# Attention values with the probabilities stationary and V moving, and queries as 512-wide matmuls, in a one-token decode block

## The chip, the core and the metric

The kernel runs on one core of a Trainium2 chip. The metric is the device time of one execution in microseconds (us). The kernel before takes 207.13 us, the median of three runs (206.97, 207.13 and 207.15).

## The reference

One token passes through a transformer block: layer norm, attention over a cache of 4096 positions with 32 heads of 128 (every query head has its own keys and values), an output projection with a residual, a second layer norm, and a gated feed-forward with GELU and a second residual. Inputs and output are bf16.

```
h  = x + attention(layernorm(x))            # x: [1, 1, 640]
q  = (layernorm(x) @ wq)                    # 32 heads x 128
p  = softmax(q . k_cache / sqrt(128))       # k_cache, v_cache: [1, 32, 4096, 128]
o  = p @ v_cache                            # 32 heads x 128
h  = x + o @ wo                             # wo: [4096, 640]
h2 = h + (gelu(n @ w_gate) * (n @ w_up)) @ w_down,   n = layernorm(h)     # 640 -> 1728 -> 640
```

The two caches are 33.5 MB each, and the weights together some 17 MB; each byte is read once.

## The kernel before

The 32 heads are taken in `NG = 8` groups of `HG = 4`. Within a group, head h owns the 32 partitions 32h to 32h+31, and each partition holds `R = 128` consecutive positions of its head. So a group's K (or V) is one tile of 128 partitions x 128 rows x 128 numbers, 4 MB, fetched by one transfer. There are two buffers for K (`kbuf`) and two for V (`vbuf`).

A class `Sched` keeps one list of operations for each engine, in the order in which the Python code calls it, and adds the semaphore waits; every engine runs its list strictly in that order. All large transfers are issued by SyncE (SP) in one list, so a transfer whose buffer is not free holds back those listed behind it. The order of the loop is this: `query(0)`, `scores(0)`, `query(1)`, `softmax(0)`, and then for g = 0 to 7: `scores(g+1)`, `query(g+2)`, `softmax(g+1)`, `values(g)`, the load of K(g+3), the load of V(g+2). The parts are:

- `query(g)` (L281, L285): for each head five matmuls multiply the normed x (`xb`, copied to 32 columns) with 128 columns of `wq`, so that the head's q stands in each of its 32 partitions; ScalarE copies the result to `qb`.
- `scores(g)`: four pieces of 32 rows. `mult` (L296, VectorE) multiplies K with q into `prod`, one of three buffers; `fold` (L305, TensorE) adds up 128 numbers to 16 by eight accumulating matmuls with the identity, 512 columns each; `red` (L312, VectorE) sums the 16 that are left. VectorE's order is mult 0, mult 1, red 0, mult 2, red 1, mult 3, red 2, red 3. The buffer of K is free (`kfree`) after mult 3.
- `softmax(g)`: the maximum over each group by way of VectorE and two small matmuls (L329 to L337), then the exponentials on ScalarE (L344) into `P4`: 128 partitions x 128 rows x 4 columns, in which only the column of the partition's own head is not zero. The sums of a partition are collected in `RS`.
- `values(g)` (L351): 128 matmuls, one for each row r. V's row (128 x 128) is the stationary operand, loaded anew each time, and the 4 columns of `P4` move; the result for four heads accumulates in 4 columns of `po`. The buffer of V is free (`vfree`) after it.

After the last group, TensorE sums `RS` (L370), VectorE inverts it (L372) and scales `po` (L407), TensorE transposes (L408), VectorE copies it out (L409), and four matmuls with `sel` bring the heads' outputs into the order of `wo` (L412). 160 matmuls with one moving column make the output projection (L422), then come the residual (L426), the second layer norm, gate and up projection (L454, 70 matmuls each, into `pg` and `pu`), GELU, and 56 matmuls of the down projection (L477).

The weights of the second half have no memory of their own: `wo` lies over `wq` (free after the last query), `wg` and `wu` over the two K buffers, `wd` over the V buffer of group 6. In SP's list the last V (group 7, in three pieces) waits for values(5), and behind it stand `wo`, `wg` (K of group 6 used), `wu` (K of group 7 used) and `wd` (values(6) done).

Of the kernel before, what the change touches and what calls it, by code (L numbers as in the profile page):

```python
# [5 lines left out]
FP32 = mybir.dt.float32  # L6
BF16 = mybir.dt.bfloat16
ALU = mybir.AluOpType
ACTF = mybir.ActivationFunctionType
AX = mybir.AxisListType  # L10

D = 640
H = 32
DH = 128
SK = 4096
DF = 1728
NC_D = D // 128
# [5 lines left out]
HG = 4  # L23
NG = H // HG
PPH = 128 // HG
R = SK // PPH
RP = 32
NP = R // RP
NFT = 13
NF = NFT + 1  # L30
WD_PARTS = (6, 4, 2, 1)

WD_COLS = []
for _n in WD_PARTS:
    _b = 128 * len(WD_COLS)
    WD_COLS += [(_b, _n, _i) for _i in range(_n)]
FREM = DF - NFT * 128

# [66 lines left out]
def bass_sequential_preLN__gqa_block_cached__glu_gated_geglu__decode_kernel(  # L105
# [12 lines left out]
    S = Sched(nc)  # L118

    def sb(name, shape, dt):  # L120
        return nc.alloc_sbuf_tensor(name, shape, dt)
# [5 lines left out]
    vbuf = [sb("vbuf%d" % i, [128, R, DH], BF16) for i in range(2)]  # L127

    def over(name, base, shape):
        return nc.alloc_sbuf_tensor_at(name, shape, BF16, offset=nc.lookup_mloc(base).addr)  # L130

    wq_sb = over("wq_sb", arena, [128, NC_D, H * DH])
# [7 lines left out]
    qb = sb("qb", [128, NG, DH], BF16)  # L140
    sc = [sb("sc%d" % i, [128, R], FP32) for i in range(2)]
    P4 = [sb("P4_%d" % i, [128, R, HG], BF16) for i in range(2)]
    RS = sb("RS", [128, H], FP32)
    mx = sb("mx", [128, NG], FP32)
    mrow = sb("mrow", [1, H], FP32)
    nb = sb("nb", [128, H], FP32)
    rz = sb("rz", [128, H], FP32)
    aT = sb("aT", [128, H], BF16)
    aH = sb("aH", [H, DH], BF16)
    aP = sb("aP", [128, H], BF16)  # L150
    x_sb = sb("x_sb", [128, NC_D], BF16)
    x32 = sb("x32", [128, NC_D], FP32)
# [1 line left out]
    sq = sb("sq", [128, NC_D], FP32)  # L154
    st = sb("st", [128, 4], FP32)
    ln = sb("ln", [128, 12], FP32)
    xb = sb("xb", [128, NC_D, PPH], BF16)
    hln = sb("hln", [128, NC_D], BF16)
    g_t = sb("g_t", [128, NF], FP32)
    t1 = sb("t1", [128, NF], FP32)  # L160
# [11 lines left out]
    ones = sb("ones", [128, 128], FP32)  # L172
    ones_bf = sb("ones_bf", [128, 128], BF16)
    I32 = sb("I32", [128, 128], FP32)
    Ibf = sb("Ibf", [128, 128], BF16)
# [4 lines left out]
    pq = nc.alloc_psum_tensor("pq", [128, 512], FP32)  # L180
    pm = nc.alloc_psum_tensor("pm", [128, 512], FP32)
    po = nc.alloc_psum_tensor("po", [128, 512], FP32)
    pz = nc.alloc_psum_tensor("pz", [128, 512], FP32)
    pg = nc.alloc_psum_tensor("pg", [128, 512], FP32)
    pu = nc.alloc_psum_tensor("pu", [128, 512], FP32)


    t_one = S.op("vector", lambda v: v.memset(ones[:, :], 1.0))
# [13 lines left out]
        e4[:, :], I32[:, :].rearrange("p (j i) -> p j i", j=4), axis=AX.X), [t_i32])  # L202
    t_m32 = S.op("vector", lambda v: v.reduce_sum(
        m32[:, :], I32[:, :].rearrange("p (j i) -> p i j", j=4), axis=AX.X))
    t_sel = None
    for j in range(4):
        t_sel = S.op("gpsimd", lambda g, j=j: g.affine_select(
# [4 lines left out]
    d_wq = S.dma("sync", "wq", lambda s: s.dma_start(  # L212
        wq_sb[:, :, :], A_wq[:, :].rearrange("(p c) n -> p c n", c=NC_D)))
# [4 lines left out]
    d_k, d_v = [None] * NG, [None] * NG  # L218
    kfree, vfree = [None] * NG, [None] * NG

    def load_k(g):
        d_k[g] = S.dma("sync", "k%d" % (g % 2), lambda s: s.dma_start(
            kbuf[g % 2][:, :, :], cache(A_k_cache, g)), [kfree[g - 2] if g >= 2 else None])
# [23 lines left out]
    def layernorm(src, t_src, o, dst, ps, beside=None):  # L247
# [19 lines left out]

    t_x32 = S.op("vector", lambda v: v.tensor_copy(x32[:, :], x_sb[:, :]), [d_x])  # L268
    t_xb = layernorm(x32, t_x32, 0, (
        xb[:, :, :], x32[:, :].unsqueeze(2).to_broadcast([128, NC_D, PPH])), pz)  # L270


    t_qb = [None] * NG

    def query(g):
        tok = None
        for hh in range(HG):
            for c in range(NC_D):
                n0 = (g * HG + hh) * DH
                last = hh == HG - 1 and c == NC_D - 1  # L280
                tok = S.op("tensor", lambda t, hh=hh, c=c, n0=n0: t.matmul(  # L281
                    pq[hh * PPH:(hh + 1) * PPH, 0:DH], xb[:, c, :], wq_sb[:, c, n0:n0 + DH],
                    start=(c == 0), stop=(c == NC_D - 1)),
                    [t_xb, d_wq, t_qb[g - 1] if g else None], token=last)
        t_qb[g] = S.op("scalar", lambda a: a.copy(qb[:, g, :], pq[:, 0:DH]), [tok])  # L285
        return tok


    fold_done, red_done = {}, {}
    t_exp, t_pv = [None] * NG, [None] * NG  # L290
    n_piece = 0
    t_qlast = None

    def mult(g, s):
        n = g * NP + s
        return S.op("vector", lambda v: v.tensor_tensor(  # L296
            out=prod[n % NPR][:, :, :], in0=kbuf[g % 2][:, s * RP:(s + 1) * RP, :],
            in1=qb[:, g, :].unsqueeze(1).to_broadcast([128, RP, DH]), op=ALU.mult),
            [d_k[g], t_qb[g], fold_done.get(n - NPR)])

    def fold(g, s, t_mult):
        n = g * NP + s
        W = 512 // RP
        for j in range(DH // W):
            fold_done[n] = S.op("tensor", lambda t, j=j: t.matmul(  # L305
                pf[n % 2][:, :], Ibf[:, :], prod[n % NPR][:, :, j * W:(j + 1) * W],
                start=(j == 0), stop=(j == DH // W - 1)),
                [t_mult, t_ibf, red_done.get(n - 2)], token=(j == DH // W - 1))

    def red(g, s):  # L310
        n = g * NP + s
        red_done[n] = S.op("vector", lambda v: v.reduce_sum(  # L312
            sc[g % 2][:, s * RP:(s + 1) * RP],
            pf[n % 2][:, :].rearrange("p (r w) -> p r w", r=RP), axis=AX.X),
            [fold_done[n], t_exp[g - 2] if g >= 2 else None])

    def scores(g):
        for s in range(NP):
            tm = mult(g, s)
            if s == NP - 1:  # L320
                kfree[g] = tm
            fold(g, s, tm)
            if s >= 1:
                red(g, s - 1)
        red(g, NP - 1)

    def softmax(g):

# [18 lines left out]
                [e, t_p4[g % 2], t_rs, t_pv[g - 2] if g >= 2 else None])  # L347

    def values(g):
        for r in range(R):  # L350
            t_pv[g] = S.op("tensor", lambda t, r=r: t.matmul(  # L351
                po[:, g * HG:(g + 1) * HG], vbuf[g % 2][:, r, :], P4[g % 2][:, r, :],
                start=(r == 0), stop=(r == R - 1)), [t_exp[g], d_v[g][r]], token=(r == R - 1))
        vfree[g] = t_pv[g]

    query(0)
    scores(0)
    query(1)
    softmax(0)
    load_k(2)  # L360
    load_v(1)
    for g in range(NG):
        if g + 1 < NG:
            scores(g + 1)
            if g + 2 < NG:
                t_qlast = query(g + 2)
            softmax(g + 1)
        if g == NG - 1:

            z = S.op("tensor", lambda t: t.matmul(pz[:, 0:H], ones[:, :], RS[:, :], start=True, stop=True),  # L370
                 [t_exp[NG - 1]])
            t_rz = S.op("vector", lambda v: v.reciprocal(rz[:, :], pz[:, 0:H]), [z])  # L372
        values(g)
        if g + 3 < NG:
            load_k(g + 3)
        if g + 2 < NG:
            load_v(g + 2)


    def pieces(slot, dst, src, cuts, waits):  # L380
# [14 lines left out]
    d_wdr = S.dma("sync", "wdr", lambda s: s.dma_start(  # L395
        wd_sb[0:FREM, NFT, :], B_w_down[NFT * 128:DF, :]), [vfree[NG - 2]])
    d_wd = []
    for i, n in enumerate(WD_PARTS):
        s0 = len(d_wd)
        tok = S.dma("sync", "wd%d" % i, lambda s, s0=s0, n=n: s.dma_start(  # L400
            wd_sb[:, s0:s0 + n, :],
            B_w_down[128 * s0:128 * (s0 + n), :].rearrange("(p i) n -> p i n", i=n)), [vfree[NG - 2]])
# [1 line left out]
    d_wd.append(d_wdr)  # L404


    a = S.op("vector", lambda v: v.tensor_mul(aT[:, :], po[:, 0:H], rz[:, :]), [t_rz, t_pv[NG - 1]])  # L407
    a = S.op("tensor", lambda t: t.matmul(pm[0:H, 0:128], aT[:, :], Ibf[:, :], start=True, stop=True), [a])  # L408
    a = S.op("vector", lambda v: v.tensor_copy(aH[:, :], pm[0:H, 0:128]), [a])  # L409
    b = None  # L410
    for j in range(4):
        b = S.op("tensor", lambda t, j=j: t.matmul(  # L412
# [6 lines left out]
    for c in range(H):  # L419
        for cc in range(NC_D):  # L420
            last = c == H - 1 and cc == NC_D - 1
            b = S.op("tensor", lambda t, c=c, cc=cc, last=last: t.matmul(  # L422
                pp[:, cc:cc + 1], wo_sb[:, c, cc::NC_D], aP[:, c:c + 1],
                start=(c == 0 and cc == 0), stop=last, skip_group_check=True),
# [19 lines left out]
    def up(ps, w, d_w, t0):  # L444
        b = None
        for c in range(NC_D):
            for s in range(NF):
                first = c == 0 and s == 0
                last = c == NC_D - 1 and s == NF - 1
                rows, cols = FREM, slice(NFT * 128, DF)  # L450
                if s < NFT:
                    b0, n, k = WD_COLS[s]
# [8 lines left out]
    a = S.op("vector", lambda v: v.tensor_copy(g_t[:, :], pg[:, 0:NF]), [t_g])  # L461
    a = S.op("vector", lambda v: v.tensor_mul(t1[:, :], g_t[:, :], g_t[:, :]), [a])
    a = S.op("vector", lambda v: v.tensor_mul(t2[:, :], t1[:, :], g_t[:, :]), [a])
    a = S.op("vector", lambda v: v.scalar_tensor_tensor(
        out=t3[:, :], in0=t2[:, :], scalar=GELU_C1, in1=g_t[:, :], op0=ALU.mult, op1=ALU.add), [a])
    a = S.op("scalar", lambda a: a.activation(e_t[:, :], t3[:, :], ACTF.Exp, scale=-2.0 * GELU_C0), [a])
    a = S.op("vector", lambda v: v.tensor_scalar(d_t[:, :], e_t[:, :], 1.0, 0.0, ALU.add, ALU.add), [a])
    a = S.op("vector", lambda v: v.reciprocal(r_t[:, :], d_t[:, :]), [a])
    a = S.op("vector", lambda v: v.tensor_mul(gu[:, :], g_t[:, :], r_t[:, :]), [a])
    t_hm = S.op("vector", lambda v: v.tensor_mul(hm[:, :], gu[:, :], pu[:, 0:NF]), [a, t_u])  # L470

    order = [NFT] + list(range(NFT))
    for i, s in enumerate(order):
        kk = FREM if s == NFT else 128
        for j in range(4):
            last = i == NF - 1
            b = S.op("tensor", lambda t, s=s, j=j, kk=kk, last=last: t.matmul(  # L477
                pd[32 * j:32 * j + 1, 0:NQ], hm[0:kk, s:s + 1], wd_sb[0:kk, s, j * NQ:(j + 1) * NQ],
                start=False, stop=last, skip_group_check=True),
# [40 lines left out]
```

## Time and profile before

| What | us |
|---|---|
| median of the runs | 207.13 |
| span of the profiled execution, first to last instruction | 205.4 |
| TensorE busy, matmuls | 135.3 (66%) |
| TensorE busy, weight loads (beside matmuls) | 78.5 (38%) |
| VectorE busy | 103.4 (50%) |
| ScalarE busy | 24.5 (12%) |
| transfers | 84.48 MB, mean 411 GB/s |
| mean granted TensorE clock | 0.790 |

The profile's own record of the execution is its span, 205.4 us; the time of a run, 207.13 us in the median, holds some 1.7 us more around the program's instructions. A step in the profile that moves the last instruction moves the time by as much. The busy time of a matmul holds its passage through the array, so matmuls that follow each other closely overlap in it; how fast they really follow is read from stretches of many.

### The profile page before, as it was taken

How to read it: one execution, taken by the hardware profiler on the slowest of the kernel's cores; microseconds unless marked ns; L12 is line 12 of the kernel's file. 1: busy time of each engine (PE TensorE's matmuls, PEld its weight loads, DVE VectorE, ACT ScalarE, POOL GpSimd, SP SyncE). 2: the span in 40 equal slices, each digit the busy share in tenths (PEclk: the TensorE clock that was granted, in tenths of full speed). 3: DMA queues.
4: the chain of work that ended last, by engine and by line, in shares of the span. 5: the costliest groups of instructions: out<-in, count | busy, mean ns of one | idle time of the engine just before them, and what ended most of it. 6: DMA issues, size and time to landing. Idle time of an engine off the chain costs nothing.

```text
span 205.4 us, 3993 instructions
## 1 busy us (share of the span) xinstructions
PE 135.3 (66%) x1847; PEld 78.5 (38%) x1847; DVE 103.4 (50%) x118; ACT 24.5 (12%) x86; POOL 2.2 (1%) x11
## 2 busy tenths in 40 slices
PE   0003049758698889684978598857777767687883
PEld 0002013223282373254326333712262237676771
DVE  2003087698685757925782777188627940001120
ACT  2001000040040050022004000500040004000000
POOL 3000000000000000000000000000000000000000
PEclk9999999978967975995599559959995995555555
DMA  7999999999999999999999999999999999999981
GB/s 247 439 431 408 434 453 440 408 434 456 427 415 424 440 440 413 421 443 426 434 421 440 424 427 434 431 437 415 440 427 431 399 422 424 423 416 422 397 336 46
DMA packets 4712, 84.48 MB, mean 411 GB/s; under 512 B 664, under 2 KB 856, under 8 KB 1880
## 3 DMA queue, kind: packets, MB, share of 16 engines
q1 hardware_dynamic: 4552, 84.23, 96.6%
q8 instruction: 14, 0.23, 0.5%
q10 hardware_dynamic: 144, 0.00, 0.0%
q14 instruction: 2, 0.02, 0.0%
HBM read 84.23 MB, written 0.00 MB: 410 GB/s over the span
## 4 chain that ended last, share of the span: by engine, by line
DMA 60%; DVE 21%; PE 13%; SPq 4%; issue 1%
DMA kbuf<-in_A_k_cache_dram 49%; DVE prod L296 16%; PE pf L305 11%; DMA wd_sb<-in_B_w_down_dram 10%; DVE sc L312 4%; SPq L400 4%; PE po L351 2%; PE pm L331 0%; PE pf L477 0%; DVE mx L329 0%; PE pz L370 0%; SPq L212 0%; PE pm L337 0%; SPq L395 0%; DVE o_sb L481 0%
## 5 line engine op out<-in xcount | busy, mean ns | idle before, releaser
L305 PE MATMUL pf<-prod,Ibf 128*128 128x512 bf16 x256 | 76.8, 461 | 33.7 <-DVE prod L296 33.6
L296 DVE TENSOR_TENSOR prod<-kbuf,qb 128x4096 bf16<-128x4096 bf16 x32 | 72.4, 2283 | 24.7 <-DMA kbuf<-in_A_k_cache_dram 24.7
L305 PEld LDWEIGHTS pf<-prod,Ibf 128*128 128x128 bf16 x256 | 27.4, 115 | 80.0 <-DVE prod L296 42.4
L312 DVE TENSOR_REDUCE sc<-pf 128x32 f32<-128x512 f32 x32 | 22.0, 688 | 24.3 <-PE pf L305 24.3
L351 PE MATMUL po<-P,vbuf 128*128 128x4 bf16 x1024 | 28.1, 165 | 2.0 <-issue 2.0
L351 PEld LDWEIGHTS po<-P,vbuf 128*128 128x128 bf16 x1024 | 27.5, 101 | 2.2 <-issue 2.1
L344 ACT ACTIVATE P<-sc,nb 32x128 bf16<-32x128 f32 x32 | 18.6, 581 | 0.9
L285 ACT CAST qb<-pq 128x128 bf16<-128x128 f32 x8 | 2.1, 265 | 103.4 <-PE pq L281 103.4
L251 PE MATMUL pz<-st,ones 128*128 128x2 f32 x4 | 1.2, 363 | 17.7 <-DVE st L250 17.7
L422 PE MATMUL pf<-aP,wo_sb 128*128 128x1 bf16 x160 | 7.0, 179 | 1.7 <-issue 1.3
L344 ACT ACTIVATION_READ_ACCUMULATOR P<-sc,nb 32x1 f32 x32 | 8.1, 254 | 0.0
L251 PEld LDWEIGHTS pz<-st,ones 128*128 128x128 f32 x4 | 1.0, 311 | 17.8 <-DVE st L250 17.8
L422 PEld LDWEIGHTS pf<-aP,wo_sb 128*128 128x128 bf16 x160 | 6.7, 131 | 2.1 <-issue 1.5
L268 DVE CAST x<-x_sb 128x5 f32<-128x5 bf16 x1 | 0.2, 172 | 14.1 <-DMA x_sb<-in_A_x_dram 14.1
L281 PE MATMUL pq<-wq_sb,xb 128*32 128x128 bf16 x160 | 5.7, 232 | 1.7 <-DVE xb L265 1.7
L331 PE MATMUL pm<-I,mx 128*1 128x128 f32 x16 | 3.0, 270 | 4.6 <-DVE mx L329 4.6
L281 PEld LDWEIGHTS pq<-wq_sb,xb 128*32 128x32 bf16 x160 | 4.2, 101 | 4.8 <-issue 3.0
L337 PE MATMUL pm<-mrow,ones 1*128 1x4 f32 x16 | 3.0, 258 | 3.0 <-DVE mrow L334 3.0
L262 ACT ACTIVATE ln<-ln 128x1 f32<-128x1 f32 x2 | 0.4, 203 | 35.1 <-DVE ln L260 35.1
L340 ACT ACTIVATE nb<-pm 128x4 f32<-128x4 f32 x8 | 1.4, 173 | 26.4 <-PE pm L337 26.4
L426 DVE TENSOR_TENSOR h<-x,pf 128x5 f32<-128x5 f32 x1 | 0.2, 161 | 8.6 <-PE pf L422 8.6
L337 PEld LDWEIGHTS pm<-mrow,ones 1*128 1x128 f32 x16 | 2.3, 182 | 5.3 <-DVE mrow L334 5.3
(59 smaller groups left out, 38.1 us busy)
## 6 DMA issues: line engine op xcount, KB each, us to landing
kbuf<-in_A_k_cache_dram SPq DMA_DIRECT2D x8, 4096.0 KB, 26.2
vbuf<-in_A_v_cache_dram SPq DMA_DIRECT2D x7, 4096.0 KB, 29.2
wq_sb<-in_A_wq_dram SPq DMA_DIRECT2D x1, 5120.0 KB, 15.4
wo_sb<-in_A_wo_dram SPq DMA_DIRECT2D x2, 1920.0 KB, 26.6
vbuf<-in_A_v_cache_dram SPq DMA_DIRECT2D x1, 2048.0 KB, 16.2
vbuf<-in_A_v_cache_dram SPq DMA_DIRECT2D x1, 1536.0 KB, 19.5
wg_sb<-in_B_w_gate_dram SPq DMA_DIRECT2D x1, 1296.0 KB, 32.8
wu_sb<-in_B_w_up_dram SPq DMA_DIRECT2D x1, 1296.0 KB, 30.1
```

What stands on the lines that cost most here:

```text
L251: c = S.op("tensor", lambda t: t.matmul(ps[:, 0:2], ones[:, :], st[:, o:o + 2], start=True, stop=True), [b, t_one])
L281: tok = S.op("tensor", lambda t, hh=hh, c=c, n0=n0: t.matmul(pq[hh * PPH:(hh + 1) * PPH, 0:DH], xb[:, c, :], wq_sb[:, c, n0:n0 + DH], star ...
L285: t_qb[g] = S.op("scalar", lambda a: a.copy(qb[:, g, :], pq[:, 0:DH]), [tok])
L296: return S.op("vector", lambda v: v.tensor_tensor(out=prod[n % NPR][:, :, :], in0=kbuf[g % 2][:, s * RP:(s + 1) * RP, :], in1=qb[:, g, :]. ...
L305: fold_done[n] = S.op("tensor", lambda t, j=j: t.matmul(pf[n % 2][:, :], Ibf[:, :], prod[n % NPR][:, :, j * W:(j + 1) * W], start=(j == 0) ...
L312: red_done[n] = S.op("vector", lambda v: v.reduce_sum(sc[g % 2][:, s * RP:(s + 1) * RP], pf[n % 2][:, :].rearrange("p (r w) -> p r w", r=R ...
L331: b = S.op("tensor", lambda t: t.matmul(pm[0:1, 0:128], mx[:, g:g + 1], I32[:, :], start=True, stop=True), [a, t_i32, t_exp[g - 1] if g el ...
L337: d = S.op("tensor", lambda t: t.matmul(pm[:, 256:256 + HG], ones[0:1, :], mrow[0:1, g * HG:(g + 1) * HG], start=True, stop=True), [c])
L344: t_exp[g] = S.op("scalar", lambda a, lo=lo, hi=hi, h=h, hh=hh: a.activation(P4[g % 2][lo:hi, :, hh], sc[g % 2][lo:hi, :], ACTF.Exp, bias= ...
L351: t_pv[g] = S.op("tensor", lambda t, r=r: t.matmul(po[:, g * HG:(g + 1) * HG], vbuf[g % 2][:, r, :], P4[g % 2][:, r, :], start=(r == 0), s ...
L400: tok = S.dma("sync", "wd%d" % i, lambda s, s0=s0, n=n: s.dma_start(wd_sb[:, s0:s0 + n, :], B_w_down[128 * s0:128 * (s0 + n), :].rearrange ...
L422: b = S.op("tensor", lambda t, c=c, cc=cc, last=last: t.matmul(pp[:, cc:cc + 1], wo_sb[:, c, cc::NC_D], aP[:, c:c + 1], start=(c == 0 and ...
```

## The change

`query(g)`: the normed x is copied to 128 columns, and five matmuls make all four heads' q at once, 512 columns wide, in all 128 partitions. ScalarE picks each head's 128 columns for its 32 partitions in four copies.

`values(g)`: the operands change places. Four rows of `P4` (128 x 16) are stationary and the four rows of V (128 x 512) move; 32 such matmuls accumulate a 16 x 512 result. Of its 16 x 4 blocks of 128 only those where the row of P equals the row of V are wanted. So there is a new step, `extract(g)`: VectorE multiplies the result with a mask (`rmask`) and sums over the four rows, and a small matmul with `gsel` (TensorE) sums the four rows' heads into 32 x 128 (`pa`), where the eight groups accumulate. `extract(g)` stands in VectorE's and TensorE's lists within scores(g+2), behind the third piece; the last two stand ahead of and behind values(7). The result has two PSUM buffers, `po` and `pg`, and `pu` becomes `pa`. The transpose at the end is gone, since the heads are rows of `pa` already, and the division by the sum becomes one scaling per head.

```diff
+VR = 4
+VM = VR * HG
...
     def query(g):
         tok = None
+        for c in range(NC_D):
+            n0 = g * HG * DH
+            tok = S.op("tensor", lambda t, c=c, n0=n0: t.matmul(
+                pq[:, :], xb[:, c, :], wq_sb[:, c, n0:n0 + HG * DH],
+                start=(c == 0), stop=(c == NC_D - 1)),
+                [t_xb, d_wq, t_qb[g - 1] if g else None], token=(c == NC_D - 1))
         for hh in range(HG):
-            for c in range(NC_D):
-                n0 = (g * HG + hh) * DH
-                last = hh == HG - 1 and c == NC_D - 1
-                tok = S.op("tensor", lambda t, hh=hh, c=c, n0=n0: t.matmul(
-                    pq[hh * PPH:(hh + 1) * PPH, 0:DH], xb[:, c, :], wq_sb[:, c, n0:n0 + DH],
-                    start=(c == 0), stop=(c == NC_D - 1)),
-                    [t_xb, d_wq, t_qb[g - 1] if g else None], token=last)
-        t_qb[g] = S.op("scalar", lambda a: a.copy(qb[:, g, :], pq[:, 0:DH]), [tok])
+            lo, hi = hh * PPH, (hh + 1) * PPH
+            t_qb[g] = S.op("scalar", lambda a, lo=lo, hi=hi, hh=hh: a.copy(
+                qb[lo:hi, g, :], pq[lo:hi, hh * DH:(hh + 1) * DH]), [tok])
         return tok
...
             if s >= 1:
                 red(g, s - 1)
+            if s == 2 and g >= 2:
+                extract(g - 2)
         red(g, NP - 1)
+
+    def extract(g):
+        a = S.op("vector", lambda v: v.tensor_tensor(
+            out=xm[:, :, :], in0=pv[g % 2][0:VM, :].rearrange("p (r d) -> p r d", r=VR),
+            in1=rmask[:, :].unsqueeze(2).to_broadcast([VM, VR, DH]), op=ALU.mult), [t_pv[g], t_gsel])
+        t_ext[g] = S.op("vector", lambda v: v.reduce_sum(
+            xz[g % 2][:, :], xm[:, :, :].rearrange("p r d -> p d r"), axis=AX.X),
+            [a, t_acc[g - 2] if g >= 2 else None])
+        t_acc[g] = S.op("tensor", lambda t: t.matmul(
+            pa[0:H, 0:DH], gsel[:, :, :].rearrange("p g x -> p (g x)")[:, g * H:(g + 1) * H], xz[g % 2][:, :],
+            start=(g == 0), stop=(g == NG - 1), skip_group_check=True), [t_ext[g]])
...
     def values(g):
-        for r in range(R):
-            t_pv[g] = S.op("tensor", lambda t, r=r: t.matmul(
-                po[:, g * HG:(g + 1) * HG], vbuf[g % 2][:, r, :], P4[g % 2][:, r, :],
-                start=(r == 0), stop=(r == R - 1)), [t_exp[g], d_v[g][r]], token=(r == R - 1))
+        n = R // VR
+        for i in range(n):
+            r = i * VR
+            t_pv[g] = S.op("tensor", lambda t, i=i, r=r: t.matmul(
+                pv[g % 2][0:VM, :], P4[g % 2][:, r:r + VR, :], vbuf[g % 2][:, r:r + VR, :],
+                start=(i == 0), stop=(i == n - 1)),
+                [t_exp[g], d_v[g][r], t_ext[g - 2] if g >= 2 else None], token=(i == n - 1))
         vfree[g] = t_pv[g]
...
-            z = S.op("tensor", lambda t: t.matmul(pz[:, 0:H], ones[:, :], RS[:, :], start=True, stop=True),
+            z = S.op("tensor", lambda t: t.matmul(pz[0:H, 0:1], RS[:, :], ones[:, 0:1], start=True, stop=True),
                  [t_exp[NG - 1]])
-            t_rz = S.op("vector", lambda v: v.reciprocal(rz[:, :], pz[:, 0:H]), [z])
+            t_rz = S.op("vector", lambda v: v.reciprocal(rz[:, :], pz[0:H, 0:1]), [z])
+            extract(NG - 2)
         values(g)
...
-    a = S.op("vector", lambda v: v.tensor_mul(aT[:, :], po[:, 0:H], rz[:, :]), [t_rz, t_pv[NG - 1]])
-    a = S.op("tensor", lambda t: t.matmul(pm[0:H, 0:128], aT[:, :], Ibf[:, :], start=True, stop=True), [a])
-    a = S.op("vector", lambda v: v.tensor_copy(aH[:, :], pm[0:H, 0:128]), [a])
+    extract(NG - 1)
+    a = S.op("vector", lambda v: v.tensor_scalar(
+        aH[:, :], pa[0:H, 0:DH], rz[:, 0:1], 0.0, ALU.mult, ALU.add), [t_rz, t_acc[NG - 1]])
```

At the start four small VectorE operations more build `rmask`, `hsel` and `gsel`, and the last step of the first layer norm writes 640 columns of `xb` in place of 160.

More of the change, by code (lines that the diff above doesn't have):

```diff
@@ L146, in bass_sequential_preLN__gqa_block_cached__glu_gated_geglu__decode_kernel @@
     nb = sb("nb", [128, H], FP32)
-    rz = sb("rz", [128, H], FP32)
-    aT = sb("aT", [128, H], BF16)
+    rz = sb("rz", [H, 1], FP32)
+    xm = sb("xm", [VM, VR, DH], FP32)
+    xz = [sb("xz%d" % i, [VM, DH], FP32) for i in range(2)]
+    rmask = sb("rmask", [VM, VR], FP32)
+    hsel = sb("hsel", [VM, HG], FP32)
+    gsel = sb("gsel", [VM, NG, H + HG], FP32)
     aH = sb("aH", [H, DH], BF16)
@@ L156, in bass_sequential_preLN__gqa_block_cached__glu_gated_geglu__decode_kernel @@
     ln = sb("ln", [128, 12], FP32)
-    xb = sb("xb", [128, NC_D, PPH], BF16)
+    xb = sb("xb", [128, NC_D, 128], BF16)
     hln = sb("hln", [128, NC_D], BF16)
@@ L185, in bass_sequential_preLN__gqa_block_cached__glu_gated_geglu__decode_kernel @@
     pu = nc.alloc_psum_tensor("pu", [128, 512], FP32)
+    pv = [po, pg]
+    pa = pu
     t_one = S.op("vector", lambda v: v.memset(ones[:, :], 1.0))
@@ L204, in bass_sequential_preLN__gqa_block_cached__glu_gated_geglu__decode_kernel @@
         m32[:, :], I32[:, :].rearrange("p (j i) -> p i j", j=4), axis=AX.X))
+    S.op("vector", lambda v: v.reduce_sum(
+        rmask[:, :], I32[0:VM, 0:VM].rearrange("p (j h) -> p j h", h=HG), axis=AX.X))
+    t_hs = S.op("vector", lambda v: v.reduce_sum(
+        hsel[:, :], I32[0:VM, 0:VM].rearrange("p (j h) -> p h j", h=HG), axis=AX.X))
+    t_gs = S.op("vector", lambda v: v.memset(gsel[:, :, :], 0.0))
+    t_gsel = S.op("vector", lambda v: v.tensor_copy(
+        gsel[:, :, 0:HG], hsel[:, :].unsqueeze(1).to_broadcast([VM, NG, HG])), [t_hs, t_gs])
     t_sel = None
@@ L269, in bass_sequential_preLN__gqa_block_cached__glu_gated_geglu__decode_kernel @@
     t_xb = layernorm(x32, t_x32, 0, (
-        xb[:, :, :], x32[:, :].unsqueeze(2).to_broadcast([128, NC_D, PPH])), pz)
+        xb[:, :, :], x32[:, :].unsqueeze(2).to_broadcast([128, NC_D, 128])), pz)
     t_qb = [None] * NG
@@ L290, in bass_sequential_preLN__gqa_block_cached__glu_gated_geglu__decode_kernel @@
     t_exp, t_pv = [None] * NG, [None] * NG
+    t_ext, t_acc = [None] * NG, [None] * NG
     n_piece = 0
```

## Prediction

> **What bounds the kernel now.** I read the page's slices first, then the chain of waits in order of time, then the timeline, and last the granted clock in stretches.
>
> ```profile
> PEclk9999999978967975995599559959995995555555
> DMA  7999999999999999999999999999999999999981
> L351 PE MATMUL po<-P,vbuf 128*128 128x4 bf16 x1024 | 28.1, 165 | 2.0 <-issue 2.0
> ```
>
> The transfers are busy in every slice but the first and the last two: the kernel streams memory, and compute lies beside it. The 1024 value matmuls are to be seen here with 28.1 us. In the chain of waits (start, us, what):
>
> ```profile
> 87.00 27.25 DMA kbuf<-in_A_k_cache_dram
> ...
> 126.06 27.05 DMA kbuf<-in_A_k_cache_dram
> 153.11 0.02 issue
> 153.13 2.30 DVE prod L296
> 155.43 0.05 issue
> 155.48 3.61 PE pf L305 x8
> 159.08 0.02 issue
> 159.11 0.69 DVE sc L312
> ...
> 168.99 3.42 PE po L351 x128
> ...
> 180.78 21.48 DMA wd_sb<-in_B_w_down_dram
> 202.26 0.04 issue
> ```
>
> K of group 5 lands at 114.24 and K of group 7 at 153.11: a group (K and V) takes the transfers (153.11 - 114.24) / 2 = 19.44 us. That is the pace to beat. The end is the last weight transfer at 202.26 and 3 us behind it. The timeline gives the matmuls' real pace, and what stands behind them:
>
> ```profile
> 162.06 1.90 PE L305 MATMUL pf<-prod,Ibf 128*128 128x512 bf16 x8 [0.74 <-DVE prod L296]
> 164.86 1.90 PE L305 MATMUL pf<-prod,Ibf 128*128 128x512 bf16 x8 [0.90 <-DVE prod L296]
> 168.92 3.49 PE L351 MATMUL po<-P,vbuf 128*128 128x4 bf16 x128
> 172.28 0.61 PE L370 MATMUL pz<-RS,ones 128*128 128x32 f32 x2
> 175.46 2.96 PE L351 MATMUL po<-P,vbuf 128*128 128x4 bf16 x105 [1.98 <-issue]
> ```
>
> Eight 512-column matmuls take 1.90 us at full clock, of which some 0.17 is the last one's passage: 0.216 us each. At half clock (155.48 above) eight take 3.61, so 0.43 each. A group's value matmuls follow each other at 3.49 / 128 = 0.027 us.
>
> **The change, part by part.** *Values.* 128 x 0.027 = 3.5 us become 32 matmuls of 512 columns. No row has 16 stationary columns. Bounds: 0.027 each (the issue pace of L351), so 0.9 us a group; and 0.43 (cold fold), so 13.7. I take 0.216, the warm fold, which has the same moving operand: 6.90 us a group.
>
> The Trainium skill, "TensorE: Matmul & The Clock Gate", section "Back-to-back issue gap", gives about 131 ns for a sustained 512-column matmul. The rows measure 216 for it; by 131 ns values would be 4.2 us and the loop 17.2, under the transfers' pace.
>
> *Extract.* No row has these two VectorE operations; both read 512 f32 in each partition, as red does (L312, 0.69, and 0.60 from start to start). Multiply 0.69, 0.02, sum 0.60 until mult 3 starts: 1.31 us. Bounds: 0.9 (the multiply at mult's 2.28 / 4096 for each number) and 1.6 (at 0.97 ns, from the xb row's 0.44 for 160 and hln's 0.29 for 5). It stands in VectorE's list between red 1 and mult 3; mult 3, fold 3, the softmax and the values behind them all come later by it. The small f32 matmul costs as L331, 0.38, and lies between fold 2 and fold 3, where TensorE waits for mult 3 anyway.
>
> *The loop.* TensorE's list closes a circle: values(g), fold 0 of g+2, and softmax(g+2), which stands ahead of values(g+1). VectorE can't run ahead of fold 0, as red 0 stands before mult 2. From the rows: fold 0 1.92 (warm, with its semaphore); from red 0's start (159.11) to the next values (168.92) 9.81; extract 1.31; values 6.90. Sum 19.94 us, over the transfers' 19.44. Before, it was 3.3 + 1.92 to 3.6 + 9.81 = 15.0 to 16.7, so TensorE waited for K. Compute now sets the pace, by half a microsecond a group; and the head start that compute has is used up at once, since the circle closes from values(0) on. That starts at 56.82 in the timeline, when the first two groups' scores are done, which the change leaves alone. So values(0) has issued its last matmul at 56.82 + 6.90 = 63.7, and values(6) at 63.7 + 6 x 19.94 = 183.4. Before it was 172.3.
>
> *Queries.* 20 matmuls in 0.67 us become five of 0.216, 1.08 us, right behind fold 3. The softmax's first matmul starts 3.0 us after fold 3 does (167.86 - 164.86), and 1.73 + 1.08 = 2.81 is inside: nothing. Four copies of 0.27 in place of one are done about 4.06 after fold 3's start, and ScalarE's next (nb, 169.03) comes 4.17 after: nothing, and only exponentials with a whole loop of room stand behind it. At the start, the wider xb (0.5 to 0.9), the query at half clock (2.2) and the copies (1.1) fall into the 6.7 us for which the first mult waits for K; the mask setup falls into the 14 us wait for x.
>
> *Between the last two groups.* The sum of RS (0.61), its reciprocal (0.16, as other one-column VectorE rows), extract(6) (0.69 + 0.02 + 0.69) and the f32 matmul's issue stand between values(6) and values(7), with some 0.1 of semaphores: 2.45 us. Values(7) runs from 185.8 to 192.7, its result is there at 192.9; before, VectorE took it up at 178.52.
>
> *Behind it.* aT and the transpose (0.57 to the start of aH) give way to extract(7) and its matmul, 0.69 + 0.02 + 0.69 + 0.04 + 0.38 + 0.04 = 1.86. L422 starts at 195.7 in place of 180.00: 15.7 later.
>
> *Given back.* Behind 180.00 compute had waited for things that will long be there: of L422's two pauses of 0.67 ("issue") one, and 0.18 for wo; 0.20 for wu; and in L477, which took 3.81 us from first to last for 0.30 + 0.97 + 1.51 of work (0.75 of that again waits), some 1.6. Together 2.65. The transfers: the last V waits for values(5), 163.4 in place of 153.0; V of group 6 lands near 153.11 + 9.7 = 162.8, so the stream stands still for a microsecond or two, and wd ends near 205, still well ahead of L477 (about 214). Nothing waits for that.
>
> Sum: 15.7 - 2.65 = 13.0, so a span of 218.4. With the 1.7 us around it, 220.2.
>
> *The clock.* The granted clock comes in stretches of multiples of 3.41 us. Fold's matmuls in such stretches (busy, weight loads, clock, share, GB/s):
>
> ```profile
> 88.31:91.72 3.41, 0.62 (x3) 0.10 (x1) 1.00 1.03 437
> 91.72:95.13 3.41, 0.00 (x0) 0.00 (x0) 0.50 1.01 432
> 146.33:149.75 3.42, 1.01 (x5) 0.28 (x3) 1.00 1.00 431
> 149.75:153.16 3.41, 0.00 (x0) 0.00 (x0) 1.00 1.01 432
> ```
>
> After a stretch with 0.62 us of wide matmuls the clock was halved; after one with 1.01 it stayed. In the new loop the thinnest 3.41 us, around the 2.35 from fold 2's end to fold 3, hold about 1.05, and those around extract(6) 0.96: just on the safe side, so it may fall now and then. A halved stretch costs half its matmul work, 1.7 us. I count one: 222.
>
> **Rivals.** *The value matmuls don't hold the clock* (only 16 of 128 columns of the array work; no row shows how that counts). For: the narrow L351 matmuls never held it, and it is 0.5 through 176 to 204 us. Against: those move 4 columns or 1, not 512. Then values cost 9 (half of them cold) to 13.7 us and a first fold 3.61: a loop of 24 to 28, seven times 4 to 8 more: 248 to 278.
>
> *The loop stays under the transfers' pace*, if a value matmul costs under 0.20: scores(7) starts at 153.13 as before, values(6) at 170.2. With 4 to 6.4 us a group, L422 starts 4 to 9 later, less the give-back: 209 to 214.
>
> *Not slower.* If 512 columns pass at near the issue pace, 0.11 each or less (3.5 us a group), L422 starts no more than 2.65 later, the wait for wd swallows it, and the end stays with the transfers: 206.7 to 207.4. For it: a quarter as many matmuls and weight loads, fewer pauses marked "issue". Against it: the folds' 0.216. It decides at 0.11.
>
> **How the numbers follow.** The loop at or above the transfers' pace with a mostly full clock: 0.72, 217 (extract at 0.9, no halved stretch) to 238 (one halved stretch in each of eight loops, 13.6, and the pauses kept, 3). The clock not held: 0.15. The loop under the pace: 0.08. Not slower: 0.05, of which faster 0.03 and same 0.02. Slower is the rest, 0.95. The range takes in parts of the neighbours: 214 to 244. About 0.2% is what this measurement can tell from no change.
>
> **What would show it.** Right: the value matmuls 32 in about 7 us; in the chain of waits no K from group 3 on, but red, mult, extract, fold, values in turn, with values(g) 20 us apart; transfers thin after 163 us; wo waiting for the heads. Wrong: value matmuls well off 0.216; a clock of 0.5 within values; K still in the chain at 114 and 153; or an extract well over 1.6.

## The result and the profile after

The changed kernel takes 225.69 us (median of six runs, 224.37 to 228.89) against 207.13: the ratio is 1.088, 95% interval 1.086 to 1.091. The prediction was 222.0 with a range of 214 to 244. The profiled execution is the slowest of the six, with a span of 227.2 us of which stretches of half clock are part (its granted clock is 0.919, that of the others 0.926 to 0.941). Runs more than 1.5% above the fastest of their kernel, this one among them, are left out of the ratios, which are of mean times; the medians take in all runs.

From the page, the granted clock and what the transfers moved in each of the 40 slices, and two groups:

```profile
PEclk9999999889999699999999999999999669697555
GB/s 274 418 421 450 444 415 433 456 415 421 459 415 415 462 407 421 453 421 415 456 427 421 441 427 427 444 421 427 107 84 420 422 430 420 426 400 232 3 3 0
L383 PE MATMUL po<-vbuf,P 128*16 128x512 bf16 x128 | 30.0, 395 | 0.0
L350 DVE TENSOR_REDUCE xz<-xm 16x128 f32<-16x512 f32 x8 | 8.1, 1010 | 0.3
```

The transfers, busy to the end before, now have a hole of two slices (107 and 84 GB/s) and end three slices before the kernel: nobody waits for them. The clock, which fell in every loop before, now stays full from the 15th slice to the 31st. The sum of extract takes 1010 ns. The chain of waits (start, us, what) shows one loop after the other, without a K after the first group's:

```profile
140.46 7.00 PE po L383 x32
...
160.84 7.00 PE pg L383 x32
167.85 1.85 PE pf L322 x8
...
169.72 0.69 DVE sc L329
170.41 2.20 DVE prod L313
172.61 0.60 DVE sc L329
173.21 0.60 DVE xm L347
...
173.83 1.02 DVE xz L350
174.84 2.21 DVE prod L313
...
177.10 3.34 PE pf L322 x8
...
182.66 8.69 PE po L383 x32
...
193.68 8.70 PE pg L383 x32
...
205.56 6.57 PE pf L456 x160
```

This is the forecast's circle, step by step: values, fold 0, red 0, mult 2, red 1, the two operations of extract, mult 3, fold 3, then the softmax and the next values 20.38 us after the last (160.84 - 140.46). The transfers keep their pace until they run out of free buffers: K of group 7 lands at 152.74, as before (153.11), but its first mult starts at 160.93, where before it started as soon as K was there (153.13). Fold 3 at 177.10 (3.34 for 1.90) and the last two values (8.7 for 7.0) show the half clock.

### The profile page after: what moved, and what is told of

Same layout as the page of the kernel before. It is cut to its first block, busy times and chain, and to the rows that moved or that the text cites. A ratio compares the mean times of both kernels' runs of the same rounds, so it can differ in the third digit from the quotient of the medians.

```text
span 227.2 us, 2290 instructions
## 1 busy us (share of the span) xinstructions
PE 162.6 (72%) x974; PEld 72.6 (32%) x974; DVE 117.1 (52%) x137; ACT 30.4 (13%) x110; POOL 2.2 (1%) x11
## 4 chain that ended last, share of the span: by engine, by line
PE 56%; DVE 30%; DMA 11%; issue 1%; ACT 1%; SPq 0%; DVEq 0%
DVE prod L313 18%; PE pf L322 16%; PE pg L383 13%; PE po L383 13%; DMA kbuf<-in_A_k_cache_dram 11%; DVE sc L329 5%; PE pq L294 4%; DVE xz L350 4%; PE pf L456 3%; DVE xm L347 2%; PE pg L488 2%; PE pu L488 2%; PE pm L361 1%; PE pm L367 1%; PE pf L511 1%
## 5 line engine op out<-in xcount | busy, mean ns | idle before, releaser
L322 PE MATMUL pf<-prod,Ibf 128*128 128x512 bf16 x256 | 65.8, 410 | 30.5 <-DVE prod L313 30.5
L383 PE MATMUL po<-vbuf,P 128*16 128x512 bf16 x128 | 30.0, 395 | 0.0
L383 PE MATMUL pg<-vbuf,P 128*16 128x512 bf16 x128 | 30.0, 395 | 0.0
L300 ACT CAST qb<-pq 32x128 bf16<-32x128 f32 x32 | 8.2, 256 | 118.0 <-PE pq L294 117.4
L383 PEld LDWEIGHTS pg<-vbuf,P 128*16 128x16 bf16 x128 | 11.6, 93 | 16.7 <-issue 2.5
L383 PEld LDWEIGHTS po<-vbuf,P 128*16 128x16 bf16 x128 | 11.6, 93 | 16.5 <-issue 2.3
L294 PE MATMUL pq<-wq_sb,xb 128*128 128x512 bf16 x40 | 11.6, 428 | 2.2 <-DVE xb L280 2.2
L350 DVE TENSOR_REDUCE xz<-xm 16x128 f32<-16x512 f32 x8 | 8.1, 1010 | 0.3
L353 PE MATMUL pu<-xz,gsel 16*32 16x128 f32 x16 | 3.2, 280 | 5.7 <-DVE xz L350 5.7
L294 PEld LDWEIGHTS pq<-wq_sb,xb 128*128 128x128 bf16 x40 | 4.2, 108 | 8.0 <-DVE xb L280 2.3
L456 PE MATMUL pf<-aP,wo_sb 128*128 128x1 bf16 x160 | 6.6, 178 | 0.3 <-DVE aP L449 0.3
L266 PEld LDWEIGHTS pz<-st,ones 128*128 128x128 f32 x4 | 1.0, 313 | 17.7 <-DVE st L265 17.7
L456 PEld LDWEIGHTS pf<-aP,wo_sb 128*128 128x128 bf16 x160 | 6.5, 131 | 0.4 <-DVE aP L449 0.4
```

The costliest lines, as they stand in the source:

```text
L294: tok = S.op("tensor", lambda t, c=c, n0=n0: t.matmul(pq[:, :], xb[:, c, :], wq_sb[:, c, n0:n0 + HG * DH], start=(c == 0), stop=(c == NC_D ...
L300: t_qb[g] = S.op("scalar", lambda a, lo=lo, hi=hi, hh=hh: a.copy(qb[lo:hi, g, :], pq[lo:hi, hh * DH:(hh + 1) * DH]), [tok])
L322: fold_done[n] = S.op("tensor", lambda t, j=j: t.matmul(pf[n % 2][:, :], Ibf[:, :], prod[n % NPR][:, :, j * W:(j + 1) * W], start=(j == 0) ...
L350: t_ext[g] = S.op("vector", lambda v: v.reduce_sum(xz[g % 2][:, :], xm[:, :, :].rearrange("p r d -> p d r"), axis=AX.X), [a, t_acc[g - 2] ...
L353: t_acc[g] = S.op("tensor", lambda t: t.matmul(pa[0:H, 0:DH], gsel[:, :, :].rearrange("p g x -> p (g x)")[:, g * H:(g + 1) * H], xz[g % 2] ...
L383: t_pv[g] = S.op("tensor", lambda t, i=i, r=r: t.matmul(pv[g % 2][0:VM, :], P4[g % 2][:, r:r + VR, :], vbuf[g % 2][:, r:r + VR, :], start= ...
```

## The experiments

The theory: since values hold TensorE for 7 us, a circle through TensorE's and VectorE's lists (values, fold 0, red 0, mult 2, red 1, extract, mult 3, fold 3, softmax) takes 20.4 us and sets the pace in place of the transfers' 19.44. Rivals: the queries are part of the loss; extract lies beside other work; the value matmuls cost their time wherever they stand; the clock. Medians stand beside the kernel before on the same chip (206.99 to 207.09).

**The queries alone** (e1), in the kernel before:

```diff
-            for c in range(NC_D):
-                n0 = (g * HG + hh) * DH
...
-                    pq[hh * PPH:(hh + 1) * PPH, 0:DH], xb[:, c, :], wq_sb[:, c, n0:n0 + DH],
+                pq[:, :], xb[:, c, :], wq_sb[:, c, n0:n0 + HG * DH],
...
-        t_qb[g] = S.op("scalar", lambda a: a.copy(qb[:, g, :], pq[:, 0:DH]), [tok])
+            t_qb[g] = S.op("scalar", lambda a, lo=lo, hi=hi, hh=hh: a.copy(
+                qb[lo:hi, g, :], pq[lo:hi, hh * DH:(hh + 1) * DH]), [tok])
```

> The kernel before with the new queries alone (five 512-wide matmuls, four copies, xb of 128 columns); values as before. Theory (the circle of values, fold 0, scores and softmax in TensorE's and VectorE's lists sets the pace, 20.4 us a group against the transfers' 19.44): the queries add at most half a microsecond to scores(1), which has copies in its way, and the later waits for K swallow it: 207.1 (206.9 to 207.4), the last weight transfer still in the chain. Rival (the queries hold up part of the loop): 208 to 211.

Measured: 207.10, ratio 1.000 (0.999 to 1.001). The queries cost nothing where the transfers set the pace.

**The values alone** (e2): the changed kernel with `query` and `xb` as before (the same diff, backwards).

> The changed kernel with the queries of before (20 matmuls of 128 columns, one copy). Theory: the loop stays at 20.4 us and the whole loss stays: about 225.2, half a microsecond of scores(1) given back (223.5 to 228, as the halved stretches fall). Rival (queries are part of it): under 222.

Measured: 224.41, ratio 1.083 (1.080 to 1.086). The loss lies with the values. Its profile has the same distance from one group's values to the next, 20.40 us:

```profile
99.63 7.00 PE po L382 x32
...
120.03 7.00 PE pg L382 x32
```

**Less extraction in the loop** (e5):

```diff
-            if s == 2 and g >= 2:
-                extract(g - 2)
...
-            start=(g == 0), stop=(g == NG - 1), skip_group_check=True), [t_ext[g]])
+            start=(g == NG - 2), stop=(g == NG - 1), skip_group_check=True), [t_ext[g]])
```

> The changed kernel without extract(0) to extract(5): six groups are left out of the sum, only the last two are masked and summed. Theory: the loop loses the whole 1.62 us that extract takes on VectorE between red 1 and mult 3, six times: 225.7 - 9.7 = 216 (214 to 218); values about 18.8 us apart. Rival (extract lies beside other work, values on TensorE alone or slower transfers are the loss): 225 to 226.

Measured: 214.30 (four runs: 211.25, 213.36 and twice 215.23), ratio 1.025 (1.019 to 1.031). In the chain of its profile:

```profile
112.15 7.00 PE pg L381 x32
...
130.91 7.00 PE po L381 x32
...
149.66 7.00 PE pg L381 x32
```

18.75 us a loop, 1.63 less than with extract: it stood in the circle with its whole time. Six loops make 9.8 us of the 11.4 between the medians. The rest fits the clock: this profile has no halved stretch up to the last values, and its span is 17.7 us shorter than the changed kernel's, 9.8 of it extract, 6.4 the half clock from values(0) on and 1.4 the earlier start of values(0).

**The extraction twice** (e6):

```diff
-                extract(g - 2)
+                extract(g - 2, masked(g - 2))
...
```

(`masked` is the same multiply and sum, once more.)

> The changed kernel with the multiply and the sum of extract(0) to extract(5) done twice. Theory: 1.62 us more in each of six loops, 225.7 + 9.7 = 235.4, and more stretches fall under the clock's bound, since the gap between folds 2 and 3 grows to 4 us: 235 to 243. Rival (extract is hidden): 225 to 227.

Measured: 246.31 (244.29 to 249.17), ratio 1.186 (1.179 to 1.193): slower than the range. The chain of its profile:

```profile
56.81 7.00 PE po L391 x32
...
142.76 0.69 DVE xm L355
...
143.47 1.01 DVE xz L358
144.48 2.21 DVE prod L313
...
146.73 3.60 PE pf L322 x8
150.33 1.71 PE pq L294 x5
...
200.10 8.29 PE po L391 x32
```

The second pass is 1.74 us (0.69 + 0.02 + 1.01 + 0.02), 10.4 in six loops. The six loops from values(0) to values(6) take 143.3 us (200.10 - 56.81) where the changed kernel's would take 6 x 20.39 = 122.3 at full clock: 21 more. The other half is the clock: the pause between folds 2 and 3 is now so long that it was halved in each loop, and fold 3 (here 3.60 for 1.90) and the query (1.71 for 1.08) ran in it. The direction was forecast, its size (up to 7.6 us) was too small.

**VectorE's list in another order** (e3):

```diff
-        for s in range(NP):
-            tm = mult(g, s)
...
+        t = mult(g, 0); fold(g, 0, t)
+        t = mult(g, 1); fold(g, 1, t)
+        t = mult(g, 2); red(g, 0); fold(g, 2, t)
+        t = mult(g, 3); kfree[g] = t; red(g, 1); fold(g, 3, t)
+        if g >= 2:
+            extract(g - 2)
+        red(g, 2); red(g, 3)
```

> The changed kernel with VectorE's list in scores reordered to mult 0, mult 1, mult 2, red 0, mult 3, red 1, extract, red 2, red 3: two mults no longer stand behind fold 0 and extract. Nothing is left out. Theory (the circle through fold 0 and red 0): after values come fold 0, red 0, mult 3, red 1, extract, red 2, red 3, 9.8 us to the next values, so a circle of 16.8 us, under the transfers' 19.44; K is back in the chain up to group 7. From K at 153.1: values(6) at 167.6, values(7) done at 184, L456 at about 187 in place of 205.6, 21.6 us more to the end: a span of 208.4, so 210 (209 to 213, a halved stretch more or less). Rival (the value matmuls and the extraction cost their own time wherever VectorE's list puts the mults): 222 to 226.

Measured: 211.94 (210.43 to 212.04), ratio 1.021 (1.017 to 1.025). The chain of its profile waits for K again:

```profile
84.53 29.30 DMA kbuf<-in_A_k_cache_dram
...
123.37 29.57 DMA kbuf<-in_A_k_cache_dram
...
167.40 7.00 PE po L388 x32
...
188.60 6.57 PE pf L461 x160
```

Not an operation is gone, the value matmuls still take 7.00 us, and 13.75 us are back. So it isn't the work that made the greater part of the loss but its order: mult 2 had stood behind a fold that stood behind values, and mult 3 behind mult 2 and the extraction. (Mult 3 still stands behind fold 0, as the new list has red 0 ahead of it; the new circle's 16.8 us can't be read off, since the loop now waits for K.) Values(6) started at 167.40, forecast 167.6. Of the profiled run's 212.04, 1.7 is a half-clock stretch in values(7) (8.71 in the profile).

**The mask of group 6 behind values(7)** (e4):

```diff
-            extract(NG - 2)
         values(g)
+        if g == NG - 1:
+            extract(NG - 2)
...
```

One wait goes with it: the multiply of extract(7) now waits for the sum of extract(6); both extracts work in `xm`.

> The changed kernel with extract(6) listed behind values(7) in place of ahead of it; nothing is left out. Theory: the hole of 2.3 us between values(6) and values(7) goes, and with it often the halved stretch that follows (values(7) took 8.7 us in the profile, 7.0 at full clock): 222.5 (221 to 224). Rival (TensorE waits there for something else, V of group 7 or the exponentials): no more than half a microsecond, 225 to 226.

Measured: 222.70 (221.96 to 223.57), ratio 1.076 (1.073 to 1.079). The hole was VectorE's work, as priced: values(7) now starts 7.04 us after values(6) in the profile, and both run at full clock:

```profile
181.47 7.00 PE po L383 x32
188.51 6.94 PE pg L383 x32
```

The hole in the changed kernel was 2.33 us (values(6) ends at 182.66 + 8.69 = 191.35, values(7) starts at 193.68); the rest of the 2.99 us between the medians was not taken apart. The sum of `RS`, which stands ahead of values(7) in every kernel here, and not behind the last group, stays in its place.

**Both edits**, e3 and e4 (e7):

> Both edits of e3 and e4 together, nothing left out. Theory: the gains add, since one lies in the loops and one behind the last of them: 208.5 (207 to 210.5). It can't get below the last weight transfer's 207. Rival as for the two.

Measured: 209.08 (208.19 to 210.04), ratio 1.009 (1.006 to 1.013). The gains add: the two alone gave 13.75 + 2.99 = 16.7, both together 16.6.

**More work for TensorE** (e9):

```diff
                 extract(g - 2)
+                filler(8)
...
+                pz[:, 0:256], Ibf[:, :], qb[:, 0:2, :], start=True, stop=True), [t_qb[1], t_ibf], token=False)
```

> The changed kernel with eight matmuls of 256 columns more in the pause between fold 2 and fold 3 of groups 2 to 7; they write a PSUM bank that nobody reads then. 0.9 us at full clock inside a pause of 1.8. Theory (a stretch of 3.41 us with less than about 0.37 of wide matmuls halves the next one): the thinnest stretch in the loops now holds over 0.55, none is halved there, and the time falls although there is more work: 224 (223 to 225), the runs closer together than before's 224.4 to 228.9. Rival (the clock is no cause of the spread, TensorE's work counts): 225.7 or slower, the same spread.

Measured: 223.13 (221.74 to 223.55), ratio 1.077 (1.073 to 1.080): 2.6 us faster with 48 matmuls more. (The 0.37 of the expectation is a share of the stretch. In the changed kernel's profile a stretch with 1.38 us of folds halved the clock and one with 1.48 did not, as shown further down; less the last matmul's passage of 0.17 these are 0.35 and 0.38 of 3.41 us.) The clock in the page's slices:

```profile
PEclk9999999979999999999999999999999999996555
```

From slice 10 to the end of the last values not a stretch is halved, and the granted clock of the four runs is 0.939 to 0.955, where the changed kernel's is 0.919 to 0.941. The loops take 20.38 us as before; what went is the half clock. That the runs lie closer together for it (1.8 us in place of 4.5) is not shown: the four runs of e2 lie within 1.4 us and those of e4 within 1.6, without the added work.

**One row of P stationary** (e8), 128 matmuls of 128 columns, so that there is no block to mask away:

```diff
-VR = 4
+VR = 1
...
-                pv[g % 2][0:VM, :], P4[g % 2][:, r:r + VR, :], vbuf[g % 2][:, r:r + VR, :],
+                pv[g % 2][0:VM, 0:VR * DH], P4[g % 2][:, r:r + VR, :], vbuf[g % 2][:, r:r + VR, :],
```

> The changed kernel with one row of P stationary in place of four (VR = 1): 128 value matmuls of 128 columns with 4 stationary columns each, as many columns moved in all, and no block to mask away; the same two VectorE operations remain, on 4 x 128 numbers. Nothing is left out. Theory (values cost the moving columns, extract its numbers in a partition): values 7.1 us a group (128 x 0.056), extract 0.45 in place of 1.62, the loop about 19.2: 214.5 (213 to 217). Rival (the number of weight loads and matmuls sets the values' time, 0.08 each or more): values 10 us, 236 or slower.

Measured: 215.93 (215.69 to 217.34), ratio 1.045 (1.041 to 1.049). Values take 7.24 us, 0.057 a matmul: four times as many matmuls and weight loads cost 0.24 us. The loop is 19.49 us (155.20 - 135.71), since extract is 0.50 (0.20 + 0.02 + 0.28):

```profile
135.71 7.24 PE po L383 x128
...
148.31 0.20 DVE xm L347
...
148.53 0.28 DVE xz L350
...
155.20 7.24 PE pg L383 x128
```

Six loops make 5.4 us of the 9.8 between the medians, and the shorter last two extractions about 2.3, as an estimate from the two profiles; the rest fits the clock, which is not halved in this profile between 47.8 and 194.5 us.

**One row and both orders** (e10):

> e8's one row together with the two orders of e7, nothing left out. Theory: extract(7) is 1.2 us shorter behind the last values, the loops lie under the transfers anyway: e7's 209.1 less 1.2, 207.9 (207.1 to 208.6); the last weight transfer is waited for again. It can't beat the kernel before, since the transfers' end stays where it is. Rival (more matmuls cost): 210 or slower.

Measured: 207.34 (207.00 to 210.09, ten runs, three of them at 208.7 or more), ratio 1.004 (1.001 to 1.008); the median is a little better than expected. In the chain of its profile:

```profile
167.38 7.24 PE po L388 x128
...
174.65 7.18 PE pg L388 x128
...
203.10 0.33 DVE o_sb L521
```

The result is copied out at 203.10, as in the kernel before (203.06). One point was missed: its chain doesn't end in a wait for the last weight; the last weight lands at 202.63, while the down projection runs from 200.91 on. No version's median came below that of the kernel before.

## Why the prediction was right

- **The bound moves from transfers to a circle through two engines' lists.** Shown: no K in the chain after the first, the last V fetched late without anybody waiting for it, and all but 2 us of the loss taken back by order alone (e3, e7).
- **Values 6.90 us.** Measured 7.00 at full clock, 0.219 each. The Trainium skill, "TensorE: Matmul & The Clock Gate", section "Back-to-back issue gap", gives about 216 ns for an isolated 512-column matmul and about 131 for a sustained stream. The streams measured here run at 219, so the sustained figure doesn't hold for them.
- **Extract 1.31 us.** Measured 1.63 in the loop: the multiply 0.60 in place of 0.69, the sum 1.01 in place of 0.60. This is the term that was mis-sized. The sum reads f32 numbers with a stride across four rows, out of SBUF, where red reads neighbours out of PSUM; which of these it is was not taken apart. The measured 1.63 lies just over the upper bound, 1.6.
- **Loop 19.94 us.** Measured 20.39: 0.32 of the 0.45 missing are extract's, 0.10 the values'.
- **The queries' copies cost nothing.** Not quite: I had looked at who stands behind them on ScalarE, and not at mult 0 of group 1, which waits for the four copies (41.80 in place of 41.31); in the timeline values(0) starts at 57.24, not at 56.82. It counts only where the circle sets the pace.
- **One stretch of half clock.** This was mis-sized: besides the one in scores(1), which the kernel before has too, the profiled execution has four, 6.4 us (1.6 between values(0) and values(1), 1.4 in the last scores, 1.7 in each of the last two values); the median is 3.2 below that execution. I had read the clock's bound from folds alone, but both stretches that I showed also held 0.67 us of queries. In the changed kernel, where no query is near, fold's busy time in stretches of the clock is this (its other matmuls in the first two of these stretches are the same two small ones):

```profile
152.70:156.12 3.42, 1.48 (x7) 0.49 (x5) 1.00 1.05 450
...
173.19:176.60 3.41, 1.38 (x7) 0.41 (x5) 1.00 1.02 434
176.60:180.02 3.42, 2.92 (x7) 1.04 (x8) 0.50 1.01 424
```

  After 1.48 us the clock stays, after 1.38 it is halved (columns: busy, weight loads, clock, share of the transfers, GB/s). With queries counted, the two stretches of before fit: 1.29 halved, 1.68 not. The bound isn't sharp, though: in the profile of e5 a stretch with 0.83 us of folds and 0.41 of values (from 165.35) kept the clock, and in that of e4 one with 1.38 of values (from 179.37). So the loop's thinnest stretch, which I had "just on the safe side", lies on either side as the stretches fall. As six of them are 20.48 us (152.70 to 173.19, within the rounding) and the loop is 20.39, they hardly shift from one group to the next.
- **Given back 2.65 us.** Measured 3.8: from L456's start to the end 21.6 us (227.2 - 205.56) in place of 25.4 (205.4 - 180.00). Both pauses of L422 are gone, not one (6.57 us in place of 8.46). The transfers' pause was mis-sized too, at no cost: I had counted a microsecond or two, and it lasts from 162.4, where V of group 6 lands, to 167.9, where values(5) is done.
- **The sum.** L456 started 9.9 us later than forecast (205.56 against 195.7): 6 loops x 0.45, 0.5 from the copies, 0.3 for each of the last two sums, and 6.4 of half clock make 10.2. The median lies 3.7 us above the forecast: loops, copies and sums are 3.8 of that and 1.2 more was given back, so as an estimate 1.1 is left for half clock beyond the one stretch counted. The mechanism was right; that the time came so near is in part errors that cancel.
- **The rivals.** That 16 columns don't hold the clock fell: values stand at full clock for 7.00 us in six groups running, and even 4 columns do (e8). The other two needed 512 columns of values in under 0.20 or 0.11 us; the changed kernel takes 0.219 for them, the one with one row 0.226 (7.24 / 32).

## What to carry to other kernels

An engine that is busy for half of the span can still set the pace when its list and another engine's wait for each other in a ring: add up the ring, not the engine, before its work is doubled. When the ring is just over the pace, look for what in it only stands there because of the order; here two mults moved up in VectorE's list, one of them out of the ring, gave back 13.75 of 18.6 us. And where four rows are taken together to save instructions, see whether the instructions cost anything: here they cost 0.24 us a group, and the wider mask cost 1.13.

## What the runs showed of the hardware that was not expected

A stretch of 3.41 us with little wide matmul work (folds, queries and values, in busy time as the profile prints it) halves the clock of the next. In these profiles, from their first clock record at 31 to 34 us on, every stretch at full clock with more than 1.38 us kept it and every one with less than 1.24 lost it. Between the two it went either way: 1.26 and 1.38 lost it in the changed kernel, 1.24 kept it in e5 and e9, and 1.38 in e4. So busy time alone doesn't decide there, and what else does is open. A kernel that lies near this bound can gain from work added in a pause: 2.6 us in e9.

What fits all of this is that moving columns count: 512-column and 128-column streams with only 16 or 4 stationary columns held the clock at full (7.00 and 7.24 us a group), while the 128 x 128 weight loads with 4 moving columns of the kernel before did not: its clock is 0.5 from 170 us on.
